# Eight reads of one PSUM bank by ScalarE ahead of VectorE's four, in place of four turns, in an attention and mixture-of-experts kernel

## The chip, the cores and the metric

One core of a Trainium2 chip. The metric is the time of one execution in microseconds on the device. TensorE (PE) multiplies and transposes, ScalarE (ACT) and VectorE (DVE) work on what it leaves in PSUM, GpSimd (POOL) on SBUF, and SyncE (SP) starts the transfers.

## What is computed

Causal attention with a compressive memory, for 4 batches, 8 heads, 576 positions and heads of 64, and then four experts of two layers, all of them used for every token and weighted by given probabilities. Scalings of the inputs are left out here.

```
scores = q @ k.T / sqrt(D), causal;   local = softmax(scores) @ v
q_p = elu(q) + 1
mem_out = (q_p @ M_prev) / (q_p . z_prev + 1e-6)
x = g * mem_out + (1 - g) * local          # g = sigmoid(beta), per head
out = sum over e of  p[:, e] * (relu(x @ w1[e]) @ w2[e])
```

x has 2304 rows (batch and position) and 512 columns (head and place in the head).

## The kernel before

**Precision.** Every operand of a matmul is split in two, a rounded high part and the rest: x = hi + lo. A product is then three matmuls (hi by hi, hi by lo, lo by hi), or two where both parts stand in one operand. ScalarE writes the high part with a copy, VectorE (or GpSimd, for weights) subtracts it from the source for the low part. The pairs are qa, qb, qpa, qpb (high and low part in the two halves of the partitions), kha and khb with kl, pth and ptl (attention weights, transposed), hh and hl (first layer), w and w2h/w2l (weights), xh and xl.

**Tasks.** A task is one batch, a pair of heads and either the first two blocks of 128 query rows ("joint" tasks) or the other rows, 256 to 575 ("later" tasks). A first group of work is written out apart; then come 12 joint tasks and, from about 195 us on, the 16 later tasks, each some 27 us long. Each task goes through slots: query block by query block, scores (`s_qk`, tile sp, masked by VectorE into s), exponential (ScalarE, L635), scaling (VectorE L651 or ScalarE L656), transposes (tile pt, evicted into pth and ptl at L660 and L662), and at a head's end the product with v and the memory (`s_o`, tile o; ScalarE's otmp and VectorE's xr bring it into the token layout).

**The experts beside it.** The expert matmuls of groups of tokens that are ready run between the pieces of the tasks: the first layer into tiles h (L876), the second into tiles y (L907, added up by VectorE into acc, L923). These are most of TensorE's work up to 660 us. From then on only the last group's experts are left. Weights come from HBM into stg, ScalarE or GpSimd makes the high part (L225, L227), GpSimd the low part (L228).

**What sets the order.** The program is written in one order by hand: a table of slots and priorities (`PR`) sets which piece of a task stands where, and a fixed rule how expert pieces are put between. Each engine then runs its own list strictly in that order; the framework puts in the waits. A PSUM bank is passed from engine to engine: where two engines read the same bank, the one that stands later in the program waits for the other's last operation on it, whatever part of the bank either reads.

**The bank of transposed queries.** `t_trq` takes a tile "to" (a tag with two banks, shared with tk, tp, o and the last piece of pt), lets TensorE transpose the query blocks and, in a later task, the last 64 keys (four transposes into tile tq), and then splits: `split_q` (ScalarE L361 and L362 write the high parts of qa and qb, VectorE L363 and L366 the low parts), `split_k` for the 64 keys (ScalarE L373 writes kha and khb, VectorE L376 kl), and four writes of the queries in another layout, qz, by ScalarE (L403). So ScalarE has eight operations on the bank and VectorE four, in the order two, two, two, two, four. `t_cpq` stands a slot behind: SP copies kha and khb to the other half of the partitions. `t_trk` does the same for the other keys (tile tk), `t_trqp` for the memory's queries (tile tp).

Of the kernel before, what the change touches and what calls it, by code (L numbers as in the profile page):

```python
# [49 lines left out]
def tile_attention_moe(  # L50
# [14 lines left out]
    P = 128  # L65
    B, H, S, D = q.shape
# [7 lines left out]
    SCALE = -1.0 / (D ** 0.5)  # L74
# [42 lines left out]
    def f(ap):  # L117
        return ap.bitcast(F32)
# [4 lines left out]
    def wid(c):  # L123
        return min((c + 1) * P, S)
# [13 lines left out]
    for i in range(2):  # L138
        o, d = i * 13 * P, {}
# [124 lines left out]
    for b, cs in RUNS[1:]:  # L264
        for a in range(NPAIR):
            t = Task()
# [85 lines left out]
    def tr(dst, src, n):  # L352
        nc.tensor.transpose(dst, src, ident[0:n, 0:n])  # L353

    def to_tile(name):
        return ps.tile([P, 512], F32, tag="to", name=name, bufs=2)

    A, Bh = slice(0, D), slice(D, P)

    def split_q(pt, qa, qb, n, scale):  # L360
        nc.scalar.activation(qa[A, 0:n], pt[A, 0:n], AF.Copy, scale=scale)  # L361
        nc.scalar.activation(qb[Bh, 0:n], pt[Bh, 0:n], AF.Copy, scale=scale)  # L362
        nc.vector.scalar_tensor_tensor(  # L363
            qa[Bh, 0:n], pt[A, 0:n], scale, f(qa[A, 0:n]), ALU.mult, ALU.subtract
        )
        nc.vector.scalar_tensor_tensor(  # L366
            qb[A, 0:n], pt[Bh, 0:n], scale, f(qb[Bh, 0:n]), ALU.mult, ALU.subtract
        )

    def split_k(pt, qk, c0, n, joint=False):  # L370
        o = slice(c0, c0 + n)
        for x, k_ in ((A, qk["kha"]), (Bh, qk["khb"])):
            nc.scalar.activation(k_[x, o], pt[x, 0:n], AF.Copy)  # L373
        for h, (x, k_) in enumerate(((A, qk["kha"]), (Bh, qk["khb"]))):
            l_ = qk["qz"][x, h * GW : h * GW + n] if joint else qk["kl"][x, o]
            nc.vector.tensor_tensor(l_, pt[x, 0:n], f(k_[x, o]), ALU.subtract)  # L376
# [9 lines left out]
    def flat(ap):  # L386
        return ap.rearrange("p j d -> p (j d)")

    def t_trq(t):
        pt = to_tile(f"tq{t.i}")  # L390
        qk, last = t.qk, t.nk == NCH
        w = len(t.cs) * P
        for i in range(len(t.cs)):

            tr(pt[:, i * P : (i + 1) * P], flat(t.nat["q"][:, i]), P)
        if last:
            tr(pt[:, w : w + P], flat(t.nat["k"][:, 4]), P)
        split_q(pt, qk["qa"], qk["qb"], w, SCALE)
        if last:
            split_k(pt[:, w:], qk, 4 * P, D)  # L400
            for h, x in enumerate((A, Bh)):
                for o, a, b_ in ((h * GW, 0, GW), (2 * GW + h * D, w - D, w)):
                    nc.scalar.activation(  # L403
                        qk["qz"][x, o : o + b_ - a], pt[x, a:b_], AF.Copy, scale=SCALE
                    )

    def t_cpq(t):
        dup_k(t.qk, 4 * P, D, copier(t))

    def t_trk(t):  # L410
        pt = to_tile(f"tk{t.i}")
        m = min(t.nk, NCH - 1)
        for c in range(m):
            tr(pt[:, c * P : (c + 1) * P], flat(t.nat["k"][:, c]), P)
        split_k(pt, t.qk, 0, m * P, t.joint)
        if t.joint:
            t_cpk(t)

    def t_cpk(t):
        dup_k(t.qk, 0, min(t.nk, NCH - 1) * P, copier(t))  # L420

    def t_trqp(t):
        pt = to_tile(f"tp{t.i}")
        if t.nk == NCH:

            tr(pt[:, t.nq - P : t.nq], flat(t.qp[:, 2]), P)
        for i in (1, 0):
            tr(pt[:, i * P : (i + 1) * P], flat(t.qp[:, i]), P)
        split_q(pt, t.qk["qpa"], t.qk["qpb"], t.nq, 1.0)
# [313 lines left out]
    for t in tasks:  # L743
# [3 lines left out]
        n = len(t.cs)  # L747
# [21 lines left out]
        )  # L769
        ev(s0 - 3, 20, lambda t=t: t_phi4(t))  # L770
        ev(s0 + PQ["trq"][0], PQ["trq"][1], lambda t=t: t_trq(t), 109.0 * n, 2 * dv(n * P))
        ev(s0 + PQ["trk"][0], PQ["trk"][1], lambda t=t: t_trk(t), 109.0 * t.nk, 2 * dv(4 * P))
        if not t.joint:
            ev(s0 + PQ["trq"][0] + 1, 0.5, lambda t=t: t_cpq(t))
# [9 lines left out]
    for i, s in slots.items():  # L784
        w = wid(s.c)
        t = s.t
# [731 lines left out]
    with tc.manual_schedule():  # L1518
# [17 lines left out]
        for g in range(1, NG + 1):  # L1536
            pt = (
                PR["frac"] * sum(pcost[: START[g] - (3 if g == 3 else 0)])
                if g < NG
                else sum(pcost[: PASS - 1]) + (PR["end"] - 1) * pcost[PASS - 1],  # L1540
                w_of(group_end[g]),
            )
# [78 lines left out]
```

## Time and profile before

| | |
|---|---|
| three runs, median (lowest to highest) | 1000.37 us (999.36 to 1000.77) |
| profiled execution: time, span | 1000.42 us, 998.6 us |
| busy: TensorE, VectorE, GpSimd, ScalarE | 98%, 65%, 59%, 57% |
| granted TensorE clock, mean | 0.998 |

The profile is that of one execution. A row of the timeline gives the start, the duration, the engine, the line of the program, the tiles written and read, and in brackets the idle time of the engine ahead of it with what ended it. A row of the waits adds up such idle times by who waited for whom. The chain of waits follows the work that ended last back through whatever released it. A stretch's granted clock is 1.00 at full speed. The recorded end of a matmul lies behind the start of the next one, since matmuls are pipelined.

### The profile page before, as it was taken

What the parts mean: (1) busy time and instruction counts of PE and PEld (TensorE: products, weight loads), DVE (VectorE), ACT (ScalarE), POOL (GpSimd) and SP (SyncE); (2) the same over time, 40 slices, a digit from 0 to 9 for tenths busy, and PEclk for the clock granted to TensorE, in tenths of its full rate; (3) what the DMA queues carried; (4) which work ended last, traced back from release to release, by engine and by line L of the source; (5) the groups of instructions that cost most, each with busy time, mean ns of one, the idle gap of its engine ahead of it and who ended that gap; (6) DMA issues with size and microseconds to landing.
All of it is one profiled execution on the core that took longest, in us unless ns stands there. A gap on an engine that the chain in (4) does not pass through costs nothing.

```text
span 998.6 us, 16042 instructions
## 1 busy us (share of the span) xinstructions
PE 983.3 (98%) x5118; PEld 824.7 (83%) x5118; DVE 650.7 (65%) x1668; ACT 565.9 (57%) x1350; POOL 593.3 (59%) x601
## 2 busy tenths in 40 slices
PE   8999999999999999999999999999999999999998
PEld 6889878877888888888888888888888888888887
DVE  6888887878877777777788787755244252442533
ACT  7687866666666677766666666554334243242430
POOL 6898856755754667756574655386363563635620
PEclk9999999999999999999999999999999999999999
DMA  6676544544443345554444433131121121111102
GB/s 166 177 196 170 142 129 122 151 118 118 127 112 100 94 139 161 149 138 115 109 126 118 106 90 87 43 127 55 51 64 43 48 59 53 54 42 53 53 1 85
DMA packets 185268, 102.16 MB, mean 102 GB/s; under 512 B 96224, under 2 KB 163552, under 8 KB 185184
## 3 DMA queue, kind: packets, MB, share of 16 engines
q1 hardware_dynamic: 184880, 101.00, 37.1%
q8 instruction: 41, 0.67, 0.3%
q14 instruction: 43, 0.35, 0.1%
q10 hardware_dynamic: 304, 0.14, 0.1%
HBM read 90.09 MB, written 4.72 MB: 95 GB/s over the span
## 4 chain that ended last, share of the span: by engine, by line
PE 82%; DVE 6%; ACT 4%; POOL 3%; issue 3%; DMA 2%; SPq 0%; POOLq 0%; ACTq 0%; DVEq 0%
PE h L876 18%; PE y L1184 17%; PE y L907 16%; PE x L1106 9%; PE z L1106 4%; PE pt L353 3%; PE o L721 3%; PE sp L611 3%; PE y L1106 2%; POOL w2l L228 1%; POOL w L228 1%; DMA stg<-in_moe_w_dram 1%; PE sp L473 1%; PE o L559 1%; DVE acc L923 1%
## 5 line engine op out<-in xcount | busy, mean ns | idle before, releaser
L228 POOL TENSOR_TENSOR w2l<-stg,w2h 128x512 fp32r<-128x512 f32 x128 | 168.0, 1316 | 152.4 <-ACT w2h L225 147.7
L876 PE MATMUL h<-xh,w 128*128 128x512 f32 (+1 forms) x768 | 246.8, 371 | 0.0
L228 POOL TENSOR_TENSOR w<-stg,w 128x512 fp32r<-128x512 f32 x96 | 127.1, 1329 | 153.5 <-ACT w L225 133.7
L876 PEld LDWEIGHTS h<-xh,w 128*128 128x128 f32 x768 | 139.3, 190 | 17.7 <-POOL w L228 0.4
L876 PE MATMUL h<-xl,w 128*128 128x512 f32 (+1 forms) x384 | 137.0, 357 | 0.0
L907 PE MATMUL y<-w2h,hh 128*128 128x512 f32 x320 | 135.8, 424 | 0.5 <-DVE hl L886 0.5
L907 PE MATMUL y<-w2l,hh 128*128 128x512 f32 x320 | 125.8, 393 | 1.0 <-POOL w2l L228 1.0
L907 PE MATMUL y<-w2h,hl 128*128 128x512 f32 x320 | 126.3, 395 | 0.0
L1201 DVE SCALAR_TENSOR_TENSOR acc<-y,pn,acc 128x512 f32<-128x512 f32 (+1 forms) x57 | 41.6, 740 | 82.2 <-PE y L1184 82.2
L876 PEld LDWEIGHTS h<-xl,w 128*128 128x128 f32 x384 | 73.2, 191 | 5.8
L660 ACT ACTIVATE pth<-pt 128x384 fp32r<-128x384 f32 (+3 forms) x128 | 49.6, 419 | 47.6 <-PE pt L353 46.7
L907 PEld LDWEIGHTS y<-w2h,hl 128*128 128x128 f32 x320 | 60.0, 188 | 14.3 <-DVE hl L886 0.8
L907 PEld LDWEIGHTS y<-w2l,hh 128*128 128x128 f32 x320 | 60.6, 189 | 10.1 <-POOL w2l L228 2.9
L885 ACT ACTIVATE hh<-h 128x512 fp32r<-128x512 f32 (+1 forms) x96 | 50.5, 526 | 32.5 <-PE h L876 31.2
L907 PEld LDWEIGHTS y<-w2h,hh 128*128 128x128 f32 x320 | 60.4, 189 | 8.6 <-DVE hl L886 0.7
L886 DVE SCALAR_TENSOR_TENSOR hl<-h,hh 128x512 fp32r<-128x512 f32 (+1 forms) x96 | 57.4, 598 | 14.0 <-ACT hh L885 12.7
L353 PE MATMUL pt<-ident,s 128*128 128x128 f32 (+1 forms) x376 | 61.2, 273 | 2.1 <-DVE ptl L662 1.0
L353 PEld LDWEIGHTS pt<-ident,s 128*128 128x128 f32 (+1 forms) x376 | 46.7, 139 | 17.5 <-PE y L907 1.8
L1130 DVE TENSOR_TENSOR cp_a<-y,cp_a 128x512 f32<-128x512 f32 x16 | 11.1, 692 | 71.4 <-PE y L1106 71.4
L225 ACT ACTIVATE w<-stg 128x512 fp32r<-128x512 f32 x92 | 57.1, 626 | 0.7
L923 DVE SCALAR_TENSOR_TENSOR acc<-y,pn,acc 128x512 f32<-128x512 f32 x70 | 52.0, 743 | 6.0 <-PE y L907 5.5
L635 ACT ACTIVATE s<-s,st 128x384 f32<-128x384 f32 (+2 forms) x80 | 54.7, 684 | 1.0 <-DVE st L619 0.7
(274 smaller groups left out, 2571.9 us busy)
## 6 DMA issues: line engine op xcount, KB each, us to landing
stg<-in_moe_w_dram SPq DMA_DIRECT2D x256, 256.0 KB, 2.9
natall<-in_k_dram SPq DMA_DIRECT2D x34, 128.0 KB, 2.6
natall<-in_v_dram SPq DMA_DIRECT2D x32, 128.0 KB, 3.1
natall<-in_q_dram SPq DMA_DIRECT2D x60, 64.0 KB, 2.7
out_dram<-acc SPq DMA_DIRECT2D x15, 256.0 KB, 2.0
kha<-kha SPq DMA_DIRECT2D x16, 128.0 KB, 2.2
khb<-khb SPq DMA_DIRECT2D x16, 128.0 KB, 2.3
natall<-in_k_dram SPq DMA_DIRECT2D x28, 64.0 KB, 2.4
```

The lines of the kernel that those rows point to most:

```text
L225: nc.scalar.activation(hi, t, AF.Copy)
L228: nc.gpsimd.tensor_tensor(lo, t, f(hi), ALU.subtract)
L353: nc.tensor.transpose(dst, src, ident[0:n, 0:n])
L635: nc.scalar.activation(s.s[:, 0:w], s.s[:, 0:w], AF.Exp, bias=s.st[:, 0:1], scale=-1.0, accum_out=s.st[:, 2:3],)
L660: nc.scalar.activation(dh, src, AF.Copy)
L876: nc.tensor.matmul(pt[0][:, cols], lhsT=w_[:, c], rhs=x_[:, c, cols], start=(c == 0 and z == 0), stop=(c == NKD - 1 and z == 2),)
L885: nc.scalar.activation(h_, pt[0][:, cols], AF.Relu)
L886: nc.vector.scalar_tensor_tensor(l_, pt[0][:, cols], 0.0, f(h_), ALU.max, ALU.subtract)
L907: nc.tensor.matmul(pt[0], lhsT=h_[fc][:, tk], rhs=w_, start=(fc == 0 and z == 0), stop=(fc == HF - 1 and z == 2),)
L923: nc.vector.scalar_tensor_tensor(acc[g, tt], pt[0], pe, acc[g, tt], ALU.mult, ALU.add)
L1106: nc.tensor.matmul(k_, lhsT=w_[:, c], rhs=x_[:, c], start=new and n == 0, stop=n == 5, skip_group_check=True,)
L1184: nc.tensor.matmul(y0, lhsT=a[:, tk], rhs=w_[:, x0:x1], start=(fc == 0 and z == 0), stop=(fc == HF - 1 and z == 2),)
```

## The change

`split_q` and `split_k` are taken apart into ScalarE's half (`q_hi`, `k_hi`) and VectorE's half (`q_lo`, `k_lo`). In a later task's `t_trq` ScalarE's halves and the four writes of qz stand first, VectorE's halves behind them. Joint tasks, `t_trqp` and `t_trk` keep their order of operations.

```diff
--- before.py
+++ after.py
@@ -358,8 +358,14 @@
     A, Bh = slice(0, D), slice(D, P)
 
     def split_q(pt, qa, qb, n, scale):
+        q_hi(pt, qa, qb, n, scale)
+        q_lo(pt, qa, qb, n, scale)
+
+    def q_hi(pt, qa, qb, n, scale):
         nc.scalar.activation(qa[A, 0:n], pt[A, 0:n], AF.Copy, scale=scale)
         nc.scalar.activation(qb[Bh, 0:n], pt[Bh, 0:n], AF.Copy, scale=scale)
+
+    def q_lo(pt, qa, qb, n, scale):
         nc.vector.scalar_tensor_tensor(
             qa[Bh, 0:n], pt[A, 0:n], scale, f(qa[A, 0:n]), ALU.mult, ALU.subtract
         )
@@ -367,10 +373,13 @@
             qb[A, 0:n], pt[Bh, 0:n], scale, f(qb[Bh, 0:n]), ALU.mult, ALU.subtract
         )
 
-    def split_k(pt, qk, c0, n, joint=False):
+    def k_hi(pt, qk, c0, n):
         o = slice(c0, c0 + n)
         for x, k_ in ((A, qk["kha"]), (Bh, qk["khb"])):
             nc.scalar.activation(k_[x, o], pt[x, 0:n], AF.Copy)
+
+    def k_lo(pt, qk, c0, n, joint=False):
+        o = slice(c0, c0 + n)
         for h, (x, k_) in enumerate(((A, qk["kha"]), (Bh, qk["khb"]))):
             l_ = qk["qz"][x, h * GW : h * GW + n] if joint else qk["kl"][x, o]
             nc.vector.tensor_tensor(l_, pt[x, 0:n], f(k_[x, o]), ALU.subtract)
@@ -395,14 +404,17 @@
             tr(pt[:, i * P : (i + 1) * P], flat(t.nat["q"][:, i]), P)
         if last:
             tr(pt[:, w : w + P], flat(t.nat["k"][:, 4]), P)
-        split_q(pt, qk["qa"], qk["qb"], w, SCALE)
+        q_hi(pt, qk["qa"], qk["qb"], w, SCALE)
         if last:
-            split_k(pt[:, w:], qk, 4 * P, D)
+            k_hi(pt[:, w:], qk, 4 * P, D)
             for h, x in enumerate((A, Bh)):
                 for o, a, b_ in ((h * GW, 0, GW), (2 * GW + h * D, w - D, w)):
                     nc.scalar.activation(
                         qk["qz"][x, o : o + b_ - a], pt[x, a:b_], AF.Copy, scale=SCALE
                     )
+        q_lo(pt, qk["qa"], qk["qb"], w, SCALE)
+        if last:
+            k_lo(pt[:, w:], qk, 4 * P, D)
 
     def t_cpq(t):
         dup_k(t.qk, 4 * P, D, copier(t))
@@ -412,7 +424,8 @@
         m = min(t.nk, NCH - 1)
         for c in range(m):
             tr(pt[:, c * P : (c + 1) * P], flat(t.nat["k"][:, c]), P)
-        split_k(pt, t.qk, 0, m * P, t.joint)
+        k_hi(pt, t.qk, 0, m * P)
+        k_lo(pt, t.qk, 0, m * P, t.joint)
         if t.joint:
             t_cpk(t)
```

The lists of the engines keep their length and their order; what differs is what an instruction waits for. ScalarE's list at the first later task, before (rows with a line number and the tiles written and read, and in brackets the engines waited for; three more writes of qz are left out):

```order
L361 ACTIVATE qa_78<-tq_2846 64x384 [waits PE_49]
L362 ACTIVATE qb_79<-tq_2846 64x384
L373 ACTIVATE kha_83<-tq_2846 64x64 [waits DVE_49]
L373 ACTIVATE khb_84<-tq_2846 64x64
L403 ACTIVATE qz_80<-tq_2846 64x256 [waits DVE_49]
L573 ACTIVATE otmp_2884<-o_2873 64x256 [waits PE_49]
```

and now:

```order
L365 ACTIVATE qa_78<-tq_2846 64x384 [waits PE_49]
L366 ACTIVATE qb_79<-tq_2846 64x384
L379 ACTIVATE kha_83<-tq_2846 64x64
L379 ACTIVATE khb_84<-tq_2846 64x64
L412 ACTIVATE qz_80<-tq_2846 64x256
L586 ACTIVATE otmp_2884<-o_2873 64x256 [waits PE_49]
```

The waits of the third and of the fifth operation for VectorE are gone.

VectorE's list at the same place, before:

```order
L363 SCALAR_TENSOR_TENSOR qa_78<-tq_2846,qa_78 64x384 [waits PE_49,Activation_49]
L366 SCALAR_TENSOR_TENSOR qb_79<-tq_2846,qb_79 64x384
L376 TENSOR_TENSOR kl_85<-tq_2846,kha_83 64x64 [waits Activation_49]
L376 TENSOR_TENSOR kl_85<-tq_2846,khb_84 64x64
L923 SCALAR_TENSOR_TENSOR acc_1_2106<-y_1_1_2827,pn,acc_1_2106 128x512 [waits PE_49]
L584 TENSOR_TENSOR xr<-o_2873,otmp_2884 64x256 [waits PE_49,Activation_49]
```

and now:

```order
L369 SCALAR_TENSOR_TENSOR qa_78<-tq_2846,qa_78 64x384 [waits PE_49,Activation_49]
L372 SCALAR_TENSOR_TENSOR qb_79<-tq_2846,qb_79 64x384
L385 TENSOR_TENSOR kl_85<-tq_2846,kha_83 64x64
L385 TENSOR_TENSOR kl_85<-tq_2846,khb_84 64x64
L936 SCALAR_TENSOR_TENSOR acc_1_2106<-y_1_1_2827,pn,acc_1_2106 128x512 [waits PE_49]
L597 TENSOR_TENSOR xr<-o_2873,otmp_2884 64x256 [waits PE_49,Activation_49]
```

The first subtraction of kl has lost its wait for ScalarE; the wait stands at the first product, L369, and by the rule of the bank it is for the last of the eight operations ahead of it in the program.

ScalarE's list in the eighth later task, with what is queued behind, before:

```order
L361 ACTIVATE qa_86<-tq_5051 64x384 [waits PE_49]
L362 ACTIVATE qb_87<-tq_5051 64x384
L373 ACTIVATE kha_91<-tq_5051 64x64 [waits DVE_49]
L373 ACTIVATE khb_92<-tq_5051 64x64
L403 ACTIVATE qz_88<-tq_5051 64x256 [waits DVE_49]
L635 ACTIVATE s_5013,st_5014<-s_5013,st_5014 128x512
L573 ACTIVATE otmp_5090<-o_5079 64x320 [waits PE_49,Activation_49]
L885 ACTIVATE hh_102<-h_1_5068 128x256 [waits PE_49]
L225 ACTIVATE w2h_112<-stg_4958 128x512 [waits DMAHW0_49,Pool_49]
```

and now:

```order
L365 ACTIVATE qa_86<-tq_5051 64x384 [waits PE_49]
L366 ACTIVATE qb_87<-tq_5051 64x384
L379 ACTIVATE kha_91<-tq_5051 64x64
L379 ACTIVATE khb_92<-tq_5051 64x64
L412 ACTIVATE qz_88<-tq_5051 64x256
L648 ACTIVATE s_5013,st_5014<-s_5013,st_5014 128x512 [waits DVE_49]
L586 ACTIVATE otmp_5090<-o_5079 64x320 [waits PE_49,Activation_49]
L898 ACTIVATE hh_102<-h_1_5068 128x256 [waits PE_49]
L225 ACTIVATE w2h_112<-stg_4958 128x512 [waits DMAHW0_49,Pool_49]
```

Behind qz stand the exponential of a slot (L635, now L648), otmp, the first layer's hh and the weights' w2h, in the same order; the exponential now names its own wait for VectorE, which qz's wait covered before.

## Rows read from the trace of the kernel before

**Rows 1.** Page, part 1: busy us, share of the span, instructions.
```profile
PE 983.3 (98%) x5118; PEld 824.7 (83%) x5118; DVE 650.7 (65%) x1668; ACT 565.9 (57%) x1350; POOL 593.3 (59%) x601
```

**Rows 2.** Waits of TensorE, 195 to 660 us: in total, times, longest us.
```profile
PE tp L353 <- ACT qz L403: 1.8, 1, 1.8
PE tp L353 <- POOL qp L345: 1.6, 1, 1.6
PE y L907 <- POOL w2l L228: 1.0, 1, 1.0
PE pt L353 <- DVE ptl L662: 1.0, 1, 1.0
PE y L907 <- DVE hl L886: 0.5, 1, 0.5
PE pt L353 <- ACT ex L308: 0.4, 1, 0.4
PE pt L353 <- ACT w2h L225: 0.4, 1, 0.4
```

**Rows 3.** Timeline, first later task: start us, us, engine, operation, idle before.
```profile
196.00 0.49 ACT L362 ACTIVATE qb<-tq 64x384 fp32r<-64x384 f32 x1
...
199.37 0.40 PE L876 MATMUL h<-xh,w 128*128 128x512 f32 x1
...
199.53 0.22 ACT L373 ACTIVATE kha<-tq 64x64 fp32r<-64x64 f32 x1 [3.04 <-DVE qb L366]
...
200.26 0.23 DVE L376 TENSOR_TENSOR kl<-tq,khb 64x64 fp32r<-64x64 f32 x1
...
200.52 0.99 ACT L403 ACTIVATE qz<-tq 64x256 fp32r<-64x256 f32 x4 [0.53 <-DVE kl L376]
...
201.61 0.41 PE L353 MATMUL tp<-ident,qp 128*128 128x128 f32 x2 [1.84 <-ACT qz L403]
...
202.33 0.86 DVE L584 TENSOR_TENSOR xr<-o,otmp 64x256 f32<-64x256 f32 x2 [1.06 <-ACT otmp L573]
```

**Rows 4.** Stretches: length and busy us by engine, granted clock (PEclk), DMA, GB/s.
```profile
203.00:204.00 1.00, 1.00 (x5) 0.76 (x4) 0.97 (x5) 0.98 (x3) 1.00 (x2) 0.50 0.39 114
...
206.00:207.00 1.00, 1.00 (x7) 0.75 (x6) 0.89 (x6) 0.05 (x1) 0.01 (x1) 0.80 0.57 137
...
422.00:426.00 4.00, 4.00 (x23) 3.40 (x22) 3.83 (x13) 2.58 (x6) 3.83 (x5) 1.00 0.55 127
```

**Rows 5.** Who waited for whom, whole span: in total, times, longest us.
```profile
ACT kha L373 <- DVE qb L366: 23.9, 16, 3.0
...
DVE qa L363 <- ACT qb L362: 7.9, 14, 1.0
```

**Rows 6.** Timeline, tenth later task.
```profile
442.58 0.22 ACT L373 ACTIVATE kha<-tq 64x64 fp32r<-64x64 f32 x1 [1.19 <-DVE qb L366]
...
443.57 0.75 DVE L921 TENSOR_SCALAR acc<-y,pn 128x512 f32<-128x512 f32 x1
...
445.88 0.57 DVE L584 TENSOR_TENSOR xr<-o,otmp 64x256 f32<-64x256 f32 x2 [1.57 <-ACT otmp L573]
```

**Rows 7.** Timeline, second later task, ScalarE.
```profile
224.95 0.22 ACT L373 ACTIVATE kha<-tq 64x64 fp32r<-64x64 f32 x1 [2.90 <-DVE qb L366]
```

**Rows 8.** Chain of waits near 388 us: start us, us, what.
```profile
388.66 0.44 DVE hl L886
...
389.14 0.96 PE y L907 x3
```

**Rows 9.** Timeline, GpSimd and ScalarE at two places.
```profile
389.03 1.30 POOL L228 TENSOR_TENSOR w2l<-stg,w2h 128x512 fp32r<-128x512 f32 x1 [4.95 <-ACT w2h L225]
...
417.12 0.63 ACT L225 ACTIVATE w<-stg 128x512 fp32r<-128x512 f32 x1
...
417.83 1.30 POOL L228 TENSOR_TENSOR w<-stg,w 128x512 fp32r<-128x512 f32 x1 [3.85 <-ACT w L225]
```

**Rows 10.** One line, L651: count, duration in ns min/median/max, first and last start.
```profile
L651 DVE TENSOR_SCALAR s<-s,st x48: 485/768/1642, 221.2 to 634.5; 128x512 f32<-128x512 f32 x32, 128x576 f32<-128x576 f32 x16
```

## The prediction

> **What bounds the kernel now.** I read the page's busy times first: TensorE is busy for 98% of the span [rows 1], so only TensorE's idle time, or a lower clock of it, can be won, and what the change saves on ScalarE or VectorE counts only where TensorE waits for it. The second view is therefore who TensorE waited for between 195 and 660 us, the stretch that holds all 16 later tasks [rows 2]. There are few such waits, each once: 1.8, 1.6, 1.0, 1.0, 0.5, 0.4 and 0.4 us, together 6.7 us. The question is which of them hang on the four turns that ScalarE and VectorE take on the bank tq. The third view is the timeline of the places themselves, and the chain of waits where a place has several links.
>
> The first later task shows the turns in full [rows 3]. ScalarE has written qa and qb by 196.49, then stands idle for 3.04 us until VectorE, which came late to the bank, has done its two; two short copies by ScalarE, two subtractions by VectorE that end at 200.49, and only then the four writes to qz (0.99 us), which end at 201.51. TensorE wants the bank for tp and stands from 199.77 to 201.61. Then the clock: 203 to 206 us runs at a granted clock of 0.50, the next microsecond at 0.80 [rows 4]. That is the 1.2 GHz level, after TensorE's idle 1.84 us; after the idle 1.6 us ahead of 421.79 it stayed at 1.00 [rows 2, 4].
>
> Over the whole run ScalarE waited 23.9 us in 16 waits for VectorE's second product [rows 5]. Nearly all of it is hidden by TensorE's own work, and I count nothing for it but the places below.
>
> **The change part by part.** No instruction is added, taken away or moved on any engine's list; the waits change. ScalarE loses two waits per later task, VectorE loses the one ahead of kl. VectorE's first product now stands in the program behind all eight ScalarE operations on its bank, and that it carries the wait for them is to be seen in the list: kl has no wait of its own left, though it reads what ScalarE's third and fourth write.
>
> In a task where VectorE is on time [rows 6]: ScalarE ended its first two at 442.58 - 1.19 = 441.39. With no turn the six others follow, 2 x 0.24 + 0.99 = 1.47 us, to 442.87. Before, kl ended at 443.54 (acc starts at 443.57), and ScalarE ended 0.03 + 0.99 later, at 444.56. So ScalarE is free 1.69 us earlier. VectorE starts at 442.90, needs 1.13 for its two products (the 1.19 that ScalarE waits, less two hand-overs of 0.03) and 0.46 for two subtractions, and ends at 444.49: 0.95 us later. That is the price. Its cover is VectorE's idle time behind the bank, 1.57 us ahead of xr here, and xr waits for ScalarE's otmp, which itself comes 1.69 us earlier; so xr starts no later than now. VectorE was on time in 13 of the 16 tasks (14 waits of qa for qb [rows 5], one of them in an early task). I count zero for these; what it costs if the cover is gone is the slow rival. The copies kha and khb by DMA wait for ScalarE's third and fourth operation and go out earlier; SP's list behind them does too. Zero.
>
> Now the places, each against its idle time.
>
> *First task* [rows 3]. ScalarE's eight end at 196.49 + 1.47 = 197.98, before VectorE is there. VectorE's products still end at 199.50 (a hand-over of 0.03 ahead of 199.53), the two subtractions follow without a turn and end at 199.99. The bank is then free 1.52 us earlier than 201.51, and TensorE's idle time falls from 1.84 to about 0.3: **1.5 us**. With so short a wait I expect the clock to hold: three microseconds at 0.50 and one at 0.80 are **1.7 us** of full speed [rows 4]. But VectorE doesn't gain that much here: 0.5 at kl and the 1.06 it idles for otmp [rows 3], 1.6 in all, against 3.2 for TensorE. The difference has to fit into slack or comes back as a new wait; I take back **0.6**, between 0 and 1.6.
>
> *Second task.* ScalarE stands for 2.90 us at the turn [rows 7], then works off a queue whose end, through VectorE's ptl, holds the next pt transposes for 1.0 us [rows 2]. ScalarE's queue starts almost 3 us earlier: **1.0**.
>
> *The two waits of 0.4 us* that end on ScalarE's queue (ex, w2h) [rows 2]. The queue is 1.7 us earlier: **0.8**.
>
> *The wait of 0.5 us for hl* [rows 8]. The chain runs from the turns to ScalarE's otmp, VectorE's xr and hl, to TensorE's y. All links shift by over 1 us: **0.5**.
>
> *The two waits for GpSimd* [rows 2, 9]. GpSimd is itself idle for 4.95 us until ScalarE's w2h, and for 3.85 us until ScalarE's w at 417.12, both queued behind the qz writes. ScalarE is free 1.7 us earlier, and so lets GpSimd start 1.7 us earlier, more than TensorE's 1.0 and 1.6: **2.6**.
>
> Sum: 1.5 + 1.7 - 0.6 + 1.0 + 0.8 + 0.5 + 2.6 = **7.5 us**. The profiled execution took 1000.42 us, 1.82 more than its span, and the median of the three runs is 1000.37; 1000.4 - 7.5 = **992.9**. Bounds: if nothing comes back, all 6.7 of rows 2 and the clock's 1.7 make 8.4. The recorded end of a matmul also overlaps the next: 0.40 us of record [rows 3] against 23 in 4.00 us, 0.17 each [rows 4]. Up to 0.2 more at each of seven waits is 1.4, in all 9.8: 990.6.
>
> **The rivals.** *GpSimd keeps its pace:* its work on the weights is held by its own queue or by the loads, not by ScalarE, and the last term (2.6) stays. For it: GpSimd still has several long operations in a row there. Against: its idle 4.95 and 3.85 us. 4.9 us gained, **995.5**.
>
> *The clock falls anyway:* it fell once, and over a microsecond after TensorE had begun again at 201.61 [rows 3, 4], so one wait need not be the whole cause. Then 1.7 is lost and the 0.6 with it: 6.4 gained, **994.0**. The Trainium skill (TensorE: Matmul & The Clock Gate, "What's actually happening") says that the gate follows how busy TensorE has been recently; by it the thin stretch, not the wait alone, would decide. The trace holds one fall and can't tell the two apart.
>
> *VectorE's scaling gets slower beside GpSimd:* L651 stands ahead of ptl, and its time runs from 485 to 1642 ns [rows 10]. Earlier, it may fall beside other GpSimd work; a loss of up to 1.16 us then eats the three waits of pt, 1.8 in all: 5.7 gained, **994.7**. The Trainium skill (SBUF — State Buffer, "Who interferes with whom") has VectorE's two-port operations and GpSimd block each other for a whole instruction. That would fit the spread of L651; it speaks against any shift of VectorE's work, and gives no sign of which way.
>
> *No effect:* the waits only change their names, because what TensorE waits for has other suppliers as late (the load of w2h, POOL's order, the transposes), or each gain is given back at the next place: **1000.4**.
>
> *Slower:* VectorE, 0.95 us later in 13 tasks, is what TensorE waits for next. It decides where a product of VectorE behind the bank is wanted less than 0.95 us after it is made now; acc at 443.57 stands directly behind the bank [rows 6]. If it held in all 13, 12.4 would be lost against 7.5 won: **1005.3**. Against it: VectorE's idle time behind the bank, and not one wait of TensorE for acc among rows 2.
>
> **How the numbers follow.** The forecast, 992.9 (own range 990.6 to 994.8), 0.55; GpSimd keeps its pace 0.14; the clock falls anyway 0.10; VectorE's scaling 0.06; no effect 0.10; slower 0.05. A measurement of this kernel can tell about 0.2%, 2 us, from no change. The first four cases are faster by more: 0.85; within 0.2%: 0.10; slower: 0.05. The range for 8 in 10 takes in those four and a partial gain behind them, with 2.5 us: 990.6 to 997.9.
>
> **What would show it.** Right: ScalarE's eight operations on tq back to back (about 2.46 us), no wait of kha for qb, VectorE's first product 2.5 us behind ScalarE's first instead of 1.0; TensorE's wait for tp near 199.7 us about 0.3 us, and named VectorE; no stretch at 0.50 near 203 us; the other waits of rows 2 gone. Wrong: new waits of TensorE for VectorE's acc, mask or hl within 5 us behind a tq bank; GpSimd's waits for ScalarE as long as now; the clock's fall at another place.

## The result, and the profile after

The changed kernel takes 990.57 us, the median of five runs (990.26 to 993.18), against 1000.37 us for the kernel before (five runs, 999.18 to 1000.77): a ratio of 0.991, interval 0.9896 to 0.9925. A second set of runs gave 992.65 against 999.46, ratio 0.9928, interval 0.9914 to 0.9941. The two intervals overlap only between 0.9914 and 0.9925, so the gain is some 8 us, between 6 and 10; the forecast was 7.5.

The page of the changed kernel, part 1 and the chain, and the chain of before:

```profile
PE 982.5 (99%) x5118; PEld 825.3 (83%) x5118; DVE 648.2 (65%) x1668; ACT 567.0 (57%) x1350; POOL 591.3 (60%) x601
...
PE 92%; DVE 3%; issue 1%; ACT 1%; DMA 1%; POOL 1%; POOLq 0%; ACTq 0%; DVEq 0%
```

```profile
PE 82%; DVE 6%; ACT 4%; POOL 3%; issue 3%; DMA 2%; SPq 0%; POOLq 0%; ACTq 0%; DVEq 0%
```

The engines do the same work in the same time as in [rows 1]. What changed is what the end hangs on: TensorE's own share of the chain went from 82% to 92%. TensorE's waits in the changed kernel between 190 and 660 us, in total, times, longest us; these two are all there are:

```profile
PE tp L353 <- DVE kl L385: 0.3, 1, 0.3
PE o L734 <- DVE ptl L675: 0.3, 1, 0.3
```

All seven waits of [rows 2] are gone; a new one of 0.3 stands where the 1.8 stood. The other 0.3, for ptl, is not new: the kernel before has it too, just ahead of 195 us. The first later task of the changed kernel, where [rows 3] showed the turns:

```profile
197.10 0.47 ACT L365 ACTIVATE qa<-tq 64x384 fp32r<-64x384 f32 x1
...
198.09 0.22 ACT L379 ACTIVATE kha<-tq 64x64 fp32r<-64x64 f32 x1
...
198.57 0.99 ACT L412 ACTIVATE qz<-tq 64x256 fp32r<-64x256 f32 x4
...
199.97 0.55 DVE L369 SCALAR_TENSOR_TENSOR qa<-tq,qa 64x384 fp32r<-64x384 f32 x1
...
201.34 0.23 DVE L385 TENSOR_TENSOR kl<-tq,khb 64x64 fp32r<-64x64 f32 x1
...
201.72 0.41 PE L353 MATMUL tp<-ident,qp 128*128 128x128 f32 x2 [0.35 <-DVE kl L385]
```

ScalarE's eight operations run in one piece, from 197.10 to 199.56, 2.46 us. VectorE comes late as before, finds them done, and its four end at 201.57; TensorE idles 0.35 us instead of 1.84. The tenth later task, where VectorE is on time ([rows 6] of before), and the waits over the whole span ([rows 5]):

```profile
433.84 0.49 ACT L366 ACTIVATE qb<-tq 64x384 fp32r<-64x384 f32 x1
...
434.83 0.99 ACT L412 ACTIVATE qz<-tq 64x256 fp32r<-64x256 f32 x4
...
435.86 0.55 DVE L369 SCALAR_TENSOR_TENSOR qa<-tq,qa 64x384 fp32r<-64x384 f32 x1 [2.38 <-ACT qz L412]
...
437.22 0.23 DVE L385 TENSOR_TENSOR kl<-tq,khb 64x64 fp32r<-64x64 f32 x1
```

```profile
DVE qa L369 <- ACT qz L412: 26.8, 14, 2.5
```

Counted from the end of ScalarE's second operation (434.33), ScalarE is free after 1.49 us (before: 3.17) and VectorE after 3.12 (before: 2.15). That is 1.68 earlier and 0.97 later; the forecast had 1.69 and 0.95. Idle time was not saved by this: ScalarE's 23.9 us of waits for VectorE became 26.8 us of VectorE's for ScalarE, where the old form of that wait had 7.9. It moved to an engine whose lateness TensorE hardly felt.

**Where the time went.** TensorE runs the same 5118 matmuls in the same order in both kernels. So the start of the n-th matmul before, less its start now, is a curve that is flat where neither kernel waits and steps up where a wait went, down where one came. The steps of two profiled executions of the changed kernel (the one shown, of 993.18 us, and one of 990.84 us from the second set) against the profiled execution of before:

| place, in us of before | forecast | shown | second |
|---|---|---|---|
| 201.6, tp of the first task | 1.5 | 1.5 | 1.5 |
| 203 to 206, clock | 1.7 | 1.5 | 1.5 |
| 219, new wait at y | -0.6 | -0.5 | -0.5 |
| 230 to 256, pt of the second task and behind | 1.0 | 1.7 | 1.7 |
| 341 and 369, the two waits of 0.4 | 0.8 | 1.2 | 1.2 |
| 376, new wait at y | none | -0.4 | -0.4 |
| 389, hl | 0.5 | 0.8 | 0.8 |
| 393 and 422, the two waits for GpSimd | 2.6 | 2.7 | 2.7 |
| 427 and behind, small ones | none | 0.4 | 0.3 |
| before 195 us | none | -1.6 | 0.7 |

Behind 195 us the steps add up to 8.8 and 8.9 us, and without the clock's to 7.3. Of the small ones, 0.2 lies behind 440 us; the first task alone (below), which changes nothing there, has it too.

### The profile page after: what moved, and what is told of

It is laid out like the page before. It is cut to its first block, busy times and chain, and to the rows that moved or that the text cites. A ratio compares the mean times of both kernels' runs of the same rounds, so it can differ in the third digit from the quotient of the medians.

```text
span 991.4 us, 16041 instructions
## 1 busy us (share of the span) xinstructions
PE 982.5 (99%) x5118; PEld 825.3 (83%) x5118; DVE 648.2 (65%) x1668; ACT 567.0 (57%) x1350; POOL 591.3 (60%) x601
## 4 chain that ended last, share of the span: by engine, by line
PE 92%; DVE 3%; issue 1%; ACT 1%; DMA 1%; POOL 1%; POOLq 0%; ACTq 0%; DVEq 0%
PE h L889 21%; PE y L920 20%; PE y L1197 18%; PE x L1119 9%; PE z L1119 4%; PE pt L353 4%; PE sp L624 4%; PE o L734 3%; PE y L1119 2%; PE o L572 1%; PE sp L486 1%; PE tk L353 1%; PE tq L353 1%; PE tp L353 1%; PE id L1458 1%
## 5 line engine op out<-in xcount | busy, mean ns | idle before, releaser
L675 DVE TENSOR_TENSOR ptl<-pt,pth 128x384 fp32r<-128x384 f32 (+1 forms) x96 | 51.5, 550 | 8.1 <-ACT pth L673 5.6
L648 ACT ACTIVATE s<-s,st 128x384 f32<-128x384 f32 (+2 forms) x80 | 54.7, 684 | 2.2 <-DVE st L632 1.9
```

Source lines behind the costliest of these rows:

```text
L648: nc.scalar.activation(s.s[:, 0:w], s.s[:, 0:w], AF.Exp, bias=s.st[:, 0:1], scale=-1.0, accum_out=s.st[:, 2:3],)
L675: nc.vector.tensor_tensor(dl, src, f(dh), ALU.subtract)
```

## The experiments

All are the changed kernel with an edit in `t_trq`; "later task" counts from 1, and `t.i` is 12 for the first.

**The first task alone, and all but the first.** The edit for the first alone; in the other kernel the first line reads `new = t.i > 12`.

```diff
+        new = t.i == 12
         q_hi(pt, qk["qa"], qk["qb"], w, SCALE)
+        if not new:
+            q_lo(pt, qk["qa"], qk["qb"], w, SCALE)
         if last:
             k_hi(pt[:, w:], qk, 4 * P, D)
+            if not new:
+                k_lo(pt[:, w:], qk, 4 * P, D)
...
-        q_lo(pt, qk["qa"], qk["qb"], w, SCALE)
-        if last:
+        if new:
+            q_lo(pt, qk["qa"], qk["qb"], w, SCALE)
             k_lo(pt[:, w:], qk, 4 * P, D)
```

> The new order in the first later task alone; the fifteen others take four turns as before. My theory (each wait of TensorE is its own, and the clock's fall near 203 us follows from the wait of 1.84 us): the wait for tp falls from 1.84 to about 0.35 us, no stretch at a granted clock of 0.50 near 203 us, a new wait of about 0.4 us near 218 us; 1.5 + 1.5 - 0.4 = 2.6 us faster than before, 997.8 us. Rival (the clock falls for the thin stretch, not for the wait): the stretch at 0.50 stays, 1.5 us faster at most, 998.9 us or more. The second task's wait for pt (1.0 us) stays, and may grow where TensorE now comes earlier than ScalarE and VectorE.

Measured: 997.72 us against 1000.16, ratio 0.9979, interval 0.9969 to 0.999. The steps are those of the first three lines of the table (1.5, 1.5, -0.5) and no others of note; TensorE's waits for GpSimd, 1.6 and 1.0, stand as in [rows 2]. The steps are as expected. But this run doesn't decide between the theory and its rival on the clock: the next kernels keep the wait and have no fall either. Of the 19 runs of the kernel before that stand beside it, only 2 have a mean clock of 0.998, so the medians hardly measure the clock's term; the interval, 1 to 3 us, takes in the sum with it and without it.

> The new order in every later task but the first. My theory: the wait of 1.84 us and the stretch at 0.50 stay as before; the other waits of TensorE go: 1.1 + 0.6 + 0.6 + 0.7 + 1.0 + 1.8 and some 0.3 of small ones, about 6 us faster than before, 994.4 us. Rival (the gains hang together, what the first task gives comes back later or is needed by the others): less than 4 us, over 996.4 us.

Measured: 992.59 us against 1000.16, ratio 0.9934, interval 0.9919 to 0.9949: 1.8 us less than expected. TensorE's waits, 190 to 660 us, and a stretch of this kernel (columns as in [rows 4]):

```profile
PE tp L353 <- ACT qz L417: 1.8, 1, 1.8
PE o L739 <- DVE ptl L680: 0.3, 1, 0.3
PE y L925 <- ACT hh L903: 0.3, 1, 0.3
```

```profile
203.00:204.00 1.00, 1.00 (x7) 0.79 (x6) 0.97 (x3) 1.00 (x5) 0.92 (x2) 1.00 1.12 288
```

The first task's 1.8 us is there again, and each later gain came without it, so the gains in the later tasks don't hang on the first. But the clock held at 1.00, although TensorE had waited as long as in the kernel before. That the fall follows this wait is thus not so in each execution. The curve against the profiled execution of before has the clock's step here too, 1.6 at 203 to 206 us, and then -0.7 at 219, where the wait for hh is new, although the first task is as before. So what is given back at 219 goes with the clock that held, not with the wait for tp that went. In the profiled execution these two make 0.9 us of the difference to the forecast, and 1.0 lies ahead of 195 us.

**The eighth and ninth task alone** (`new = t.i in (19, 20)`, the rest of the edit as above), for the waits at 389 to 422 us.

> The new order in the eighth and ninth later task alone. My theory (GpSimd waits there for ScalarE's copies of the weights, which are queued behind the writes of qz): the waits for hl, w2l and qp go, 0.7 + 1.0 + 1.8, with a small one behind them 0.2: 3.7 us faster than before, 996.7 us. Rival (GpSimd keeps its own pace): only the wait for hl goes, 0.7 us, 999.7 us.

Measured: 995.97 us against 1000.16, ratio 0.9963, interval 0.9948 to 0.9977. The steps at these places are 0.8 (hl), 0.9 and 1.8 (GpSimd) and 0.2. The rival that GpSimd keeps its own pace would have left the 1.0 and the 1.8 standing; it falls. In each of two tasks VectorE's two turns are taken out of ScalarE's way, and nothing else; that releases GpSimd. The steps at 203 to 206 and at 219 us are here as well, 1.6 and -0.7, with the first task's wait of 1.8 in place.

**The last five tasks alone** (`new = t.i >= 23`), where TensorE waited for nobody before.

> The new order in the last five later tasks alone, where TensorE has no wait in the trace of before (105.00 us busy of the 105 from 500 to 605). My theory: ScalarE is free 1.7 us earlier and VectorE 0.95 us later in each, and nothing of it is seen: 1000.4 us, within 0.5. Rival (each task gives its share of the gain): 5/16 of 9, 2.8 us faster, 997.6 us.

Measured: 999.74 us, ratio 0.9999, interval 0.9989 to 1.0008: no effect. Here ScalarE's idle time goes the same way, with nothing to win from it. In this execution too, the first task's wait of 1.8 left the clock at 1.00, and the wait for hh at 219 us is there (steps 1.6 and -0.7):

```profile
PE tp L353 <- ACT qz L417: 1.8, 1, 1.8
...
PE y L925 <- ACT hh L903: 0.3, 1, 0.3
```

```profile
203.00:204.00 1.00, 1.00 (x7) 0.82 (x6) 0.95 (x5) 0.96 (x3) 1.00 (x1) 1.00 0.32 81
```

**Three turns.** VectorE's products stay in second place, and ScalarE's kha, khb and qz join behind them. Of ScalarE's two waits only the second goes, qz's for kl; kl now waits for qz.

```diff
         q_hi(pt, qk["qa"], qk["qb"], w, SCALE)
+        q_lo(pt, qk["qa"], qk["qb"], w, SCALE)
         if last:
...
-        q_lo(pt, qk["qa"], qk["qb"], w, SCALE)
-        if last:
             k_lo(pt[:, w:], qk, 4 * P, D)
```

> Order on the bank in every later task: ScalarE's qa and qb, VectorE's two products, ScalarE's other six, VectorE's two subtractions; one turn less for each engine than before, but ScalarE's wait for VectorE's products stays. My theory (what counts is when ScalarE is free): ScalarE is free only 0.5 us earlier; the wait of 1.84 us and the clock's fall stay, since the bank is released as late as before; 0.4 to 0.5 us at each of the six other places, about 2.8 us faster than before, 997.6 us. Rival (the number of turns counts, whichever they are): half of the full gain, 4.9 us, 995.5 us.

Measured: 999.33 us against 1000.41, ratio 0.9988, interval 0.9977 to 0.9999: less than either theory gave it. Who waited for whom, whole span, TensorE's longest two waits between 190 and 660 us, and the stretch behind the first of them (columns as in [rows 4]):

```profile
DVE kl L385 <- ACT qz L413: 24.6, 16, 1.5
ACT kha L379 <- DVE qb L372: 23.9, 16, 3.0
```

```profile
PE tp L353 <- DVE kl L385: 1.9, 1, 1.9
PE pt L353 <- DVE ptl L674: 1.3, 1, 1.3
```

```profile
203.00:204.00 1.00, 1.00 (x5) 0.70 (x4) 0.97 (x5) 0.94 (x4) 1.00 (x2) 0.50 0.55 167
```

ScalarE's 23.9 us for VectorE's products are untouched. Only the 0.53 for kl is taken from ScalarE's way, and VectorE now idles for qz in the middle of the bank. TensorE's 1.84 in the first task became 1.9 for kl, pt's 1.0 became 1.3, and the clock fell as in the profile of before. The curve gains 1.2 us behind 195 us, of the changed kernel's 8.8. So by difference it is the first turn that costs, the one at which ScalarE stands while VectorE comes and does its two long products. A kernel without this turn alone was not run.

**How much later VectorE may be.** The changed kernel with VectorE's two products done twice, 0.98 us more work per later task by VectorE's busy time (663.8 us against 648.2, in 16 tasks). The second writing repeats the values of the first.

```diff
         q_lo(pt, qk["qa"], qk["qb"], w, SCALE)
         if last:
+            q_lo(pt, qk["qa"], qk["qb"], w, SCALE)
             k_lo(pt[:, w:], qk, 4 * P, D)
```

> The changed kernel with VectorE's two products written twice in every later task, so that VectorE ends its part of the bank 1.1 us later still (2.1 us later than before the change). My theory (VectorE's delay is covered by its idle time behind the bank): up to 1.5 us slower than the changed kernel, 990.6 to 992, with the wait for tp in the first task grown by 1.1 us to about 1.5. Rival (VectorE's products behind the bank are wanted soon): 1.1 us in most tasks, 12 us or more slower, over 1002 us.

Measured: 996.79 us, ratio to before 0.9965, interval 0.9949 to 0.9981; so 4 to 6 us more than the changed kernel. Both theories missed: the cover is neither whole nor gone. TensorE's waits, 190 to 660 us:

```profile
PE pt L353 <- DVE ptl L676: 1.7, 4, 0.5
PE tp L353 <- DVE kl L385: 1.6, 1, 1.6
PE y L921 <- DVE hl L900: 0.7, 2, 0.4
PE o L735 <- DVE ptl L676: 0.3, 1, 0.3
```

One wait repeats what was seen in the first task (0.35 grown to 1.6, where VectorE comes last); the other six are of 0.4 us or so each. So a lateness of 0.97 us behind the bank fits under VectorE's idle time nearly everywhere, and one of about 2 shows in seven places. The changed kernel's margin on VectorE is under 1 us there.

**ScalarE's freed time taken back.** Four copies more by ScalarE behind its eight operations, in the changed kernel (598.2 us busy against 567.0, so 1.95 per later task); what they write is used by nobody.

```diff
         if last:
             k_hi(pt[:, w:], qk, 4 * P, D)
...
+        for _ in range(4 if last else 0):
+            nc.scalar.activation(t.ex, t.nat["q"], AF.Copy)
         q_lo(pt, qk["qa"], qk["qb"], w, SCALE)
```

> The changed kernel with four more copies on ScalarE (128x384, about 0.44 us each, into a tile that is free) behind its eight operations, 1.8 us in every later task, so that ScalarE is free for its queue as late as before the change; the bank and VectorE don't wait for them. My theory (ScalarE's freed time is what removed the waits for pt, hl, w2l and qp): the first task keeps its gain of the wait for tp and the clock, 2.6 us, and most of the other 6 us come back: 996 to 998 us. Rival (the turns on the bank themselves cost the time): no slower than the changed kernel, 990.6 to 991.5 us.

Measured: 999.81 us, ratio to before 0.9986, interval 0.9977 to 0.9996. TensorE's waits, 190 to 660 us:

```profile
PE y L922 <- POOL w2l L228: 1.0, 1, 1.0
PE y L922 <- DVE hl L901: 0.9, 1, 0.9
PE tp L353 <- POOL qp L345: 0.8, 1, 0.8
PE pt L353 <- ACT w2h L225: 0.7, 1, 0.7
PE y L922 <- ACT hh L900: 0.6, 2, 0.3
PE pt L353 <- ACT ex L308: 0.4, 1, 0.4
PE tp L353 <- DVE kl L385: 0.4, 1, 0.4
PE o L736 <- DVE ptl L677: 0.3, 1, 0.3
```

Of the waits of [rows 2] five are back, those for w2l, hl, qp, w2h and ex, some shorter and some longer than before, and waits for hh have come. So the gain at these places hangs on ScalarE being free earlier. Two stay away. In the first task it was VectorE's order and not ScalarE's queue. In the second task the wait of 1.0 for ptl does not return, and the curve keeps 1.1 us there. The four copies run from 222.93 to 225.13, and ScalarE is free 3.71 us after the end of its second operation (221.42), against 4.87 before (222.05 to 226.92) and 1.48 in the changed kernel: because VectorE had come so late to this bank, the copies take back only part of what the change gives. The cost of the whole was larger than expected. The 1.95 us are more than the 1.68 that the change frees, and VectorE's 0.97 stays to be paid, which would explain it but was not tried apart.

**The changed kernel once more.**

> The changed kernel once more, unaltered, to see how far its gain and the state of the clock near 203 us repeat from one execution to another. The theory (the turns' waits are gone, each time): 990.3 to 992, TensorE's only waits in 190 to 660 us are the two of 0.3 on VectorE, and no stretch at half clock behind the first later task. The rival, that part of the gain was a chance of that one set of runs (the clock, or the start of the run): 993 or more, or a stretch at half clock near 203 us that is back though the wait before it is short.

Measured: 992.65 us against 999.46, half a microsecond above what the theory gave and not up to the rival. Its profile has the same two waits of 0.3, no stretch at half clock, and the same steps behind 195 us (last column of the table). What differs from the first set is ahead of 195 us and between executions.

## Why the prediction was right, and where it was not

**The price and the freed time** came out as worked out from one task's rows: 0.97 and 1.68 us against 0.95 and 1.69. A hand-over of the bank from engine to engine costs a few hundredths; what a turn costs is the other engine's work, and its coming late.

**The places.** Each of the seven waits went. For tp, and for the five that came back when ScalarE's time was taken back, the experiments show the reasons given; the second task's wait for ptl was not tried by itself. *First task:* 1.5 against 1.5, and the wait that stays is named VectorE. *GpSimd:* 2.7 against 2.6; its idle time ahead of w2l, 4.95 in [rows 9], is now 3.27, shorter by the 1.68 that ScalarE gained:

```profile
383.94 1.30 POOL L228 TENSOR_TENSOR w2l<-stg,w2h 128x512 fp32r<-128x512 f32 x1 [3.27 <-ACT w2h L225]
```

That was the largest term and had the strongest rival; the eighth and ninth task alone settled it. *hl:* 0.8 against 0.5.

**Terms that were too small.** In these rows the recorded idle time of a matmul understates its delay: the two waits of 0.4 gave 1.2 together, the wait of 0.5 for hl 0.8, the second task's 1.0 gave 1.7 with two smaller steps behind it, at 234 and 252 to 256. The prediction had this as a bound only (up to 0.2 more at each wait) and not in its sum. Against it stands a new wait of 0.4 at 376, which the prediction did not have.

**The clock** is the step that does not stand as it was put. The stretch at half clock of [rows 4] is gone from each profile of the changed kernel, and that is a step of 1.5 us against the one profiled execution of before. But the prediction took the fall as a thing that the kernel before has. In the 48 timed runs of before beside the experiments, only 6 have the mean granted clock of 0.998 that goes with it in the profiled execution; the others have 0.999 or 1.000, and so the medians hold hardly any of it. The 0.6 given back was put down to VectorE, which gains less than TensorE in the first task. It measured 0.5 in the changed kernel and 0.7 in the three kernels that keep the wait and hold the clock, so it belongs to the clock's term.

Against an execution of before without the fall both terms go, and the prediction's own sum for that case is 6.4, as in its rival that the clock falls anyway. What the change gives there can be read off the last five alone, which up to 500 us is such an execution: between 195 and 440 us the curve of the changed kernel gains 7.9 us on it. So the total of 7.5 was right by two errors against each other, and that is luck: 1.1 us net for a fall that most executions don't have, and other terms 1.5 us too low. The waits and their owners, which make up the rest, were right for their reasons.

**What caused the fall** stays open in part. It is in two profiles (before, and three turns), both with a wait of 1.8 or 1.9 us for tp. With the same wait it is not in three others (all but the first, eighth and ninth, last five). By the mean clock of the timed runs, 11 of 76 runs of kernels with that wait have 0.998, and none of 35 of kernels in which it is 1.6 us or shorter. The six runs of before with 0.998 take 1001.5 us in the mean, the other 33 of the same two sets 1000.0, a difference of the size of the stretch in [rows 4]; where in those runs the clock fell is not on record. The wait seems to be needed and is not enough. The Trainium skill (TensorE: Matmul & The Clock Gate, "What's actually happening") says that the gate's windows run on freely and don't begin with the kernel. By that the same wait could cost the clock in one execution and not in another, which agrees with these counts; no run here shows the windows.

**The rivals.** GpSimd's own pace fell (eighth and ninth task). No effect, and slower for VectorE's sake, fell with the result: TensorE's only new waits for VectorE are 0.35 at tp and some 0.2 for hl at 219, behind 0.3 for ScalarE's hh. The step of 0.4 at 376 is no wait for VectorE: the product with w2l starts there at 372.18 us, right behind GpSimd's w2l, which runs from 370.82 to 372.12. But VectorE done twice shows that this rival is a real mechanism: the point from which the waits for ptl, hl and kl begin lies between the 0.97 us of the change and the 1.95 of that kernel. That VectorE's scaling would get slower beside GpSimd left no trace in TensorE's waits for pt; none is left in the changed kernel.

**The rest of the difference** is ahead of 195 us, where the change does nothing: 1.6 us lost in one profiled execution of the changed kernel, 0.7 won in the other. The prediction gave it no range of its own. The gains of the two sets by their medians, 9.8 and 6.8 us, lie on either side of the curve's 7.9. Such differences ahead of 195 us are large enough to be the reason, which is not shown run by run. The low end of the range, 990.6, lies just above the median of the first set, 990.57, and well under that of the second.

## What to carry to other kernels

Where two engines read one bank in turns, group each engine's reads, and put first the engine whose queue others wait behind; the turn itself is nearly free, and what it costs is the first engine standing until the second comes. Take the gain from the places where the busiest engine waits, one by one (here seven, 6.7 us of TensorE's waits beside 24 us of ScalarE's idle time), and follow each back to the queue that sets it, also through a third engine. A stretch that one profile shows, as the clock's fall here, is to be looked for in the other executions too before it goes into a sum against a median.

## What the runs showed of the hardware that was not expected

**The start of the run takes two lengths.** The first matmuls of the changed kernel, in the execution shown and in the second one:

```profile
5.84 1.65 PE L1294 MATMUL pf<-tw,tw 64*128 64x128 f32 x8 [0.61 <-DVE tw L1283]
...
8.19 2.05 PE L1458 MATMUL id<-hh 128*128 128x512 f32 x4
```

```profile
5.51 0.93 PE L1294 MATMUL pf<-tw,tw 64*128 64x128 f32 x8 [0.61 <-DVE tw L1283]
...
6.78 1.34 PE L1458 MATMUL id<-hh 128*128 128x512 f32 x4
```

The same eight matmuls took 1.65 and 0.93 us, the same four 2.05 and 1.34. A stretch of this time is printed with a granted clock of 1.00 in both, but that stands for no record: the clock's records begin only at 10.56 us in the first trace and at 4.30 in the second, at 1.00 each. The slow pace ends where they begin. It is the pace of the half-clock stretch of before: there matmuls of 128x512 start 0.43 us apart (204.31, 204.74, 205.16, 205.59), and here too (8.76, 9.19, 9.62). So the long form looks like a later rise of the clock to 1.00. Three of ten profiled executions (of kernels that are alike up to 195 us) have it, with records from 9.94 us or later; in the other seven they begin between 4.30 and 5.45. What sets it was not tried. The two profiles of the changed kernel are 2.1 us apart by it at 12 us, and 2.3 before the change begins.

**The clock's fall is not in each execution**, at the same wait of 1.8 us before it, as told above.
